# A written order for TensorE: wq's first rows by ScalarE's queue, q first, 19 exponential buffers and another list

## The chip, the cores and the metric

One core of one Trainium2 chip. Its engines are TensorE (PE in the profile, its weight loads PEld), VectorE (DVE), ScalarE (ACT), GpSimd (POOL) and SyncE (SP), which issues most transfers. The metric is the device time of one execution in microseconds, the median of several runs.

## The reference

```python
a = einsum("bsd,ed->bse", x, dft_hid_re);  b = einsum("bsd,ed->bse", x, dft_hid_im)
y = einsum("ts,bse->bte", dft_seq_re, a) - einsum("ts,bse->bte", dft_seq_im, b)
q = (x @ wq) in 32 heads of 20;  k = x @ wk;  v = x @ wv          # one k and v for all heads
p = softmax(q @ k.T * 20**-0.5);  o = (p @ v) @ wo
g = sigmoid((x * gate_w).sum(-1));  out = g * y + (1 - g) * o      # x: 2048 x 640, fp32
```

A Fourier mixing of x and an attention with 32 query heads over one shared key and value, mixed by a gate per row.

## The kernel before

All products of the first stages, of y and of o split their fp32 operands in a high and a low part (`split`) and take three products for one. The stages on TensorE are these.

1. Fifteen warm-up products (`WARM`), then `x @ [wk wv gate_w]` (tile `kv`, from `kvg`) and `x @ wq` (tile `q`), in four blocks of 512 rows of x. The first block goes chunk by chunk of 128 input features (index c): its loads alternate x and wq on SP's queue, ScalarE makes the high parts (`xh`, `wqh`), VectorE the low ones (`xl`, `wql`).
2. The hidden DFT (tile `ab`, 64 row halves, two products side by side on the two halves of the rows), with the first part of the attention's first pass between.
3. The main stage, in the order of a string `PLAN` that is written out by hand. It has three kinds of work: y, the sequence DFT, in seven products of a Strassen scheme (letters 0 and 1: the next product on the lower or the upper half of TensorE's rows); the attention's scores (letters, see below), a lower and an upper head of a pair side by side; and `V`, a step of `av`, four products of exponentials with the values on the whole of the rows. `-` empties y's bank. A letter of `SCORES` stands for a kind (a to f: first pass on the lower half, A to F: first pass on the upper half, g to l and G to L: second pass likewise) and for one of six PSUM banks.
4. A final loop for the last y groups and the rest of the second pass, then `o @ wo` with the gate and the output.

The first pass (`a_unit`) computes scores, and VectorE takes their row maxima (`mx`). When both heads of a pair are through, `a_reduce` and `a_final` come one and two ticks later, a tick being given at every second first-pass score of the list. `a_final` turns the maxima (`mt`, VectorE), splits them (`ms`, GpSimd), writes them to DRAM (`m_d`) and reads them back by four transfers into two extra rows per head of `qs`, the lower head's two first. The second pass (`b_unit`) multiplies with these rows, so its scores come with the maximum taken off; ScalarE makes the exponentials into one of 16 buffers (`pt`), which `pick` chooses while the program is built, and a step of `av` frees four of them.

SP's order is found by a scheduler; TensorE, ScalarE, VectorE and GpSimd follow the program's order. GpSimd (late in the kernel VectorE) sums and splits the DFT matrix (`split_c`).

For the last stage `load_o(n)` loads a block of 256 rows of `oT_d` and of the reciprocals `rx_d`, `mult_o` multiplies them on GpSimd, `split_o` splits them, and `o_group` takes the products.

Of the kernel before, what the change touches and what calls it, by code (L numbers as in the profile page):

```python
# [8 lines left out]
F32 = mybir.dt.float32  # L9
# [8 lines left out]
P = 128  # L18
# [12 lines left out]
WARM = 15  # L31
# [3 lines left out]
def kernel(  # L35
# [60 lines left out]

    nc.scalar.activation(gate, ident[:, :NT], AF.Exp)
# [64 lines left out]
    with ExitStack() as c1:  # L162
# [4 lines left out]
        nc.gpsimd.dma_start(kvg, wkvg.rearrange("(c p) n -> p c n", p=P))  # L167
# [590 lines left out]
    ptfree = [(-1, k) for k in range(16)]  # L758
# [82 lines left out]
    def finish_last(ts, sm):  # L841
# [20 lines left out]
        "B0A00K00F00CBjVV1e1g11d11l1c11h1e11a1j111f1h111c1-kJVHa1l1e11c1d11h11a1l11k1VHcDlAeVVCh1d1l11g1e11h1"
        "1c1l11d11gVHe0I0F00G0D00B0VIeGfDhVVhE0I0A00F00J000H0E00I00A0J000F0H00K00C0A00J0B00L00E0I000D0A000L0B"
        "iVVElj11c1g11b1l11e11d11i11g11h1l1e11c1-VdEaHcLVVDh1e1l11g1c11h111d1l11k1a111c1h11d111l1k1a1Hc1VLdKh"
        "AcVVfH0D0K00G0I00B00F0K00D0VVkAH00C00L0J00E0G00B00C00L00E0J000B00G0F00I00J00E00A0B0I00lDVVKc1a1l11h1"
        "1d1k11c1f11a111h11d1k11i1-VVBfKaIjVBk1i1f11j1a11k11h11c11l11d11a11k11h1c1f11d11KgVHkCfGdVVB00K00G0C0"
        "0L00D0B0K00G00I0F0D000E00B0A00LiVVDlI00E00H00A0L0J000C00E0H00A0L000C0D00BkVVFgIk1d111b1g11f11c1j111k"
        "1h111a1f11j1V-CaKbJlVk11c1j11a11l1h11e11c1d1GlV1e1h11c1g11d1l11e11b1iGVD0fIeB0A0VVJc0L0E000H0G00D00I"
        "00F0K00B0DgVVF00I00B0K00G0D00F00I00H0E00G00J00C0F00B0E000G0iJV1l1a11h1c11j11e11f1g11b1iDVVeGiFhJVe11"
        "fAi1b11j1-VIej11l11a111b1i1e111j1a1l11h11c1j11k11l1a11b1VcJaKlBVVdL0I0E00A0H00L00D0I00K0VViB0K0A0F00"  # L870
        "J00I00H00E0A000J0F0I00K00H00D00A000I0F00E0D00B0gCVV1f1g11e1j11b1i111l1a11k11d11i1h11f-AVVdKfIaHVdK1f"
        "1i11h11a11k1d1i11l111b1g11e1d11i11f1h111aKViDfBkAVViD00K0F00H0G00C0D00K0F000B0IaVViEJ00F0H00G00C0E00"
        "J0F00H000I00A000J0E00H0F00I00A0D00kHVVFh1c1g11e1j11b111l1a11i1j111e1l11h1VaE-cJfHVVaJ1e1h11i1l11d1g1"
        "11b11k1c1d111l1b11a111i11e1LjVIlBaDeVVlC0B0G00J0E0F00C00G0H00D0VVkA00L0B00I00D0Eg0L000B00I0D00G00K0F"
        "00C0H00G000J0K00F00B0CaVVj11f11k1b11i11a11j11lk111i11b1d11-GfVVKbIgDlVbKi11d11a11l1k11b11i1j111f1a11"
        "1k11b1i11d11l1eGVbDcFaKVVhED00I00L00A0H00E000I0J00L00B0A000I0E000J0H00F0aIVVjEF00H0A00I000J0E00H0F00"
# [24 lines left out]
        "E0G00C000F00J0E00H00I00A0J0L00B00E0C000gJVVJb1f1k11a1i111j1h111e1f11c111a1j11kHVFcJeGbVV-Fj1c11g1e1h"
        "111j1f11g1i11b1k111d11f111a1i11h1kDVfAiBkDVViFA00K0H00J00C0F00E0G00B000I0D00FaVVE00I00B0J00F00G0K00C"
        "0B00J00G00L0E00C0D000H00A0kFVVc11h1e11j1a11l11i11b1e11d1f11gi11h1-VeGdIhLVVaIh11e1l111d11i111a1h11e1"
        "1l1d11i1a11b1f111k1IjVVJaK00B00I0F00J00G0E00H00I00FdVEgFhDiVVGeF00H0D0i0G000E0H00F0I00D00G000H0E00I0"
        "0LA000J00HE00C0AfVV1e1j11c11h1a11l1k11d11i1h111a11f1kDVIhKa-LdVVi11gBdKf1VIb1g1d11k11f1c11h11g111j1e"
# [185 lines left out]
```

## Time and profile before

| | |
|---|---|
| time, median of 3 runs | 1775.57 us (1775.42 to 1776.12) |
| the profiled execution | 1775.38 us, its span 1773.6 us |
| busy: PE, PEld | 1766.9 us, 1263.0 us |
| busy: DVE, ACT, POOL | 1422.8 us, 1186.8 us, 820.1 us |
| mean granted clock of TensorE | 1.00 |

Times in the profile run from the span's start. Matmuls overlap, their ends are modelled, and the two halves of TensorE's rows work side by side, so two starts on the same half say more than a duration. A row "x4" merges several instructions. "<-" behind an idle time names what ended it.

### The profile page before, as it was taken

To read this page: it belongs to the slowest core of one execution; us is meant where nothing else is said; L and a number is where in the kernel's file an instruction comes from. 1 tells how busy PE (TensorE), PEld (TensorE's weight loads), DVE (VectorE), ACT (ScalarE), POOL (GpSimd) and SP (SyncE) were. 2 spreads that over 40 slices of the span, in tenths; PEclk is the share of its full clock that TensorE was granted. 3 is DMA by queue.
4 is the path that set the end of the run, shared out by engine and by line. 5 is a ranking of instruction groups with operands and counts; after the bars stand their busy time and mean duration, and the time that the engine had idled before them with its cause. 6 is when DMAs were issued, how large, how long until landed. Compare 5 with 4: busy or idle time off the path is not lost.

```text
span 1773.6 us, 40756 instructions
## 1 busy us (share of the span) xinstructions
PE 1766.9 (100%) x16354; PEld 1263.0 (71%) x16354; DVE 1422.8 (80%) x2335; ACT 1186.8 (67%) x2327; POOL 820.1 (46%) x560
## 2 busy tenths in 40 slices
PE   9999999999999999999999999999999999999999
PEld 7799986666666666666666666666666666667789
DVE  4469999888888898888888888888888898854344
ACT  4422247777777777777777777777777777777731
POOL 1001227454455465655766565565654454442242
PEclk9999999999999999999999999999999999999999
DMA  8762324333334442524544444353443242325666
GB/s 269 234 196 93 118 98 133 108 130 100 114 111 152 115 134 93 173 92 146 171 136 131 156 130 133 100 151 106 141 140 113 86 121 85 105 69 188 196 223 208
DMA packets 130393, 243.87 MB, mean 137 GB/s; under 512 B 25716, under 2 KB 76916, under 8 KB 127684
## 3 DMA queue, kind: packets, MB, share of 16 engines
q1 hardware_dynamic: 129356, 237.89, 42.7%
q0 software_dynamic: 848, 3.38, 0.6%
q8 instruction: 128, 2.10, 0.5%
q14 instruction: 61, 0.50, 0.1%
HBM read 194.62 MB, written 50.86 MB: 138 GB/s over the span
## 4 chain that ended last, share of the span: by engine, by line
PE 98%; DMA 1%; DVE 0%; ACT 0%; SPq 0%; issue 0%; POOL 0%; POOLq 0%; DVEq 0%; ACTq 0%
PE av L798 27%; PE y L655 21%; PE b L784 17%; PE a L329 17%; PE ab L122 7%; PE o L111 1%; PE o L112 1%; PE o L113 1%; PE q L111 1%; PE q L113 1%; PE q L112 1%; DMA x_d<-both 0%; DMA ql_d<-ql 0%; DMA kvg<-in_wkvg_dram 0%; PE kv L210 0%; PE kv L211 0%
## 5 line engine op out<-in xcount | busy, mean ns | idle before, releaser
L336 DVE TENSOR_REDUCE mx<-a 128x1 f32<-128x512 f32 x2048 | 1265.0, 683 | 171.0 <-PE a L329 111.7
L794 ACT ACTIVATE pt<-b 128x512 f32<-128x512 f32 x2048 | 1052.1, 618 | 327.1 <-PE b L784 194.8
L655 PE MATMUL y<-x,ch 64*128 64x320 f32 x3584 | 757.8, 309 | 0.0
L329 PE MATMUL a<-ks,qs 60*128 60x512 f32 x2048 | 736.2, 422 | 0.2 <-DVE mx L336 0.2
L784 PE MATMUL b<-qs,ks 62*128 62x512 f32 x2048 | 706.0, 421 | 0.5 <-ACT pt L794 0.3
L655 PEld LDWEIGHTS y<-x,ch 64*128 64x128 f32 x3584 | 559.3, 185 | 22.1 <-issue 9.4
L655 PE MATMUL y<-x,cl 64*128 64x320 f32 x1792 | 514.3, 308 | 0.0
L798 PE MATMUL av<-pt,vsb 128*32 128x512 f32 x4096 | 502.9, 600 | 0.0
L329 PEld LDWEIGHTS a<-ks,qs 60*128 60x128 f32 x2048 | 350.0, 184 | 128.0 <-DVE mx L336 98.3
L784 PEld LDWEIGHTS b<-qs,ks 62*128 62x128 f32 x2048 | 340.1, 184 | 130.3 <-ACT pt L794 70.8
L458 POOL TENSOR_TENSOR craw<-craw 128x1024 f32<-128x1024 f32 x80 | 191.2, 2390 | 269.3 <-DMA craw<-in_cre_dram 113.6
L655 PEld LDWEIGHTS y<-x,cl 64*128 64x128 f32 x1792 | 307.9, 184 | 3.8 <-issue 2.5
L798 PEld LDWEIGHTS av<-pt,vsb 128*32 128x32 f32 x4096 | 106.6, 108 | 201.1 <-issue 179.4
L463 POOL TENSOR_TENSOR cl<-craw,ch 128x1024 fp32r<-128x1024 f32 x98 | 234.6, 2394 | 7.9
L462 POOL CAST ch<-craw 128x1024 fp32r<-128x1024 f32 x98 | 101.7, 1038 | 143.4 <-PE y L655 120.2
L122 PE MATMUL ab<-wh,xh 64*128 64x320 f32 x640 | 137.0, 307 | 0.2 <-DVE both L533 0.2
L122 PE MATMUL ab<-wl,xh 64*128 64x320 f32 x640 | 136.7, 306 | 0.0
L122 PE MATMUL ab<-wh,xl 64*128 64x320 f32 x640 | 136.4, 305 | 0.0
L532 ACT ACTIVATE half<-ab 128x320 f32<-128x320 f32 x64 | 28.1, 439 | 115.4 <-PE ab L122 111.4
L711 POOL TENSOR_TENSOR ya<-yt,ya 128x320 f32<-128x320 f32 x64 | 57.4, 912 | 97.5 <-ACT yt L684 96.8
L122 PEld LDWEIGHTS ab<-wh,xl 64*128 64x128 f32 x640 | 99.7, 184 | 0.0
L122 PEld LDWEIGHTS ab<-wl,xh 64*128 64x128 f32 x640 | 99.5, 185 | 0.0
(89 smaller groups left out, 1077.2 us busy)
## 6 DMA issues: line engine op xcount, KB each, us to landing
craw<-in_cre_dram SPq DMA_DIRECT2D x96, 512.0 KB
craw<-in_cim_dram SPq DMA_DIRECT2D x96, 512.0 KB
xr<-x_d SPq DMA_DIRECT2D x88, 320.0 KB
qs<-qh_d SPq DMA_DIRECT2D x64, 160.0 KB
x_d<-both SPq DMA_DIRECT2D x64, 160.0 KB
ya<-y_d SPq DMA_DIRECT2D x64, 160.0 KB
y_d<-ya SPq DMA_DIRECT2D x64, 160.0 KB
xr<-in_xT_dram SPq DMA_DIRECT2D x20, 256.0 KB
```

The source lines that it names most:

```text
L111: nc.tensor.matmul(ps, wh, xh, start=(i == 0), stop=False)
L122: nc.tensor.matmul(ps, w[r], x[r], start=(i == 0 and k == 0), stop=(i == n - 1 and k == 2))
L329: nc.tensor.matmul(ps, qs[p][b : b + 60, qb * P : (qb + 1) * P], ks[b : b + 60, c * ROW : (c + 1) * ROW], start=True, stop=True,)
L336: return nc.vector.tensor_reduce(mx[p][:, hh, qb, c : c + 1], ps, axis=AX.X, op=ALU.max)
L458: eng.tensor_tensor(raw, raw, raws[1], op=PRODUCTS[n][0][1])
L462: eng.tensor_copy(h, raw)
L463: eng.tensor_tensor(l, raw, h.bitcast(F32), op=ALU.subtract)
L655: mm = nc.tensor.matmul(ps[g % len(ps)], w, x, start=start, stop=stop)
L711: nc.gpsimd.tensor_tensor(ya, yt, ya, op=how)
L784: nc.tensor.matmul(ps, ks[b : b + 62, kc * P : (kc + 1) * P], qs[p][b : b + 62, qc * ROW : (qc + 1) * ROW], start=True, stop=True,)
L794: halves.scored(nc.scalar.activation(t, ps, AF.Exp, scale=SCALE), n)
L798: nc.tensor.matmul(ps[32 * g : 32 * g + 32, :], vsb[:, kc, :], t, start=first, stop=last)
```

## The change

In the first stage, wq's first chunk is loaded by ScalarE's queue, ahead of the early Exp; kvg is loaded by SP's queue behind x's first chunk, in place of GpSimd's. wqh and wql are made ahead of kvg's halves, and q's products stand ahead of kv's. Twelve warm-up products instead of fifteen. There are 19 buffers of exponentials instead of 16, and `PLAN` is another string of the same length, with the same number of letters of each kind. The reciprocals of odd blocks no longer have a tile of their own: those of block 1 go in two halves into `xr0` and `xr1`, with two multiplications, those of blocks 3, 5 and 7 into `ab71`.

```diff
--- before.py
+++ after.py
@@ -28,7 +28,7 @@
 SJ = NT // 2
 SCALE = float(DH) ** -0.5
 ROW = 512
-WARM = 15
+WARM = 12
 @with_exitstack
@@ -94,8 +94,6 @@
     gate = const.tile([P, NT], F32, name="gate")
     omg = const.tile([P, NT], F32, name="omg")
-    nc.scalar.activation(gate, ident[:, :NT], AF.Exp)
-
     def words(ap):
         return ap.bitcast(F32) if ap.dtype == F32R else ap
@@ -164,7 +162,6 @@
         x1 = c1.enter_context(tc.tile_pool(name="x1", bufs=2, side="right"))
         rot = Rot(["B", "V", "F", "B", "F", "A", "A", "A"])
         kvg = w1.tile([P, KC, 41], F32, name="kvg")
-        nc.gpsimd.dma_start(kvg, wkvg.rearrange("(c p) n -> p c n", p=P))
         kvgs = w1.tile([P, KC, P], F32R, name="kvgs")
@@ -246,21 +243,24 @@
         wqraw = w2.tile([P, KC, D], F32, tag="wl1", name="wqraw")
+        move(wqraw[:, 0], wq_v[:, 0], nc.scalar)
+        nc.scalar.activation(gate, ident[:, :NT], AF.Exp)
         load_x1(0, 0)
+        move(kvg, wkvg.rearrange("(c p) n -> p c n", p=P))
         pkv = rot("kv_0")
         pq = [rot(f"q_0_{m}") for m in range(KC)]
         for c in range(KC):
             if c:
                 load_x1(0, c)
-            move(wqraw[:, c], wq_v[:, c])
+                move(wqraw[:, c], wq_v[:, c])
         for c in range(KC):
             split_x1(0, c)
+            split(wqraw[:, c], wqh[:, c], wql[:, c])
             if c == 0:
                 split(kvg, kvgs[:, :, :41], kvgs[:, :, 64:105])
-            split(wqraw[:, c], wqh[:, c], wql[:, c])
-            kv_mm(pkv, 0, c)
             for m in range(KC):
                 q_mm(pq[m], 0, m, c)
+            kv_mm(pkv, 0, c)
         for c in range(KC):
             load_x1(1, c)
         for c in range(KC):
@@ -576,17 +576,26 @@
         if n < NO:
             oraw[n] = []
             for k, v in enumerate((oT_v, rx_v)):
-                if (n % 2, k) == (1, 1):
-                    t = op.tile([P, KC, TW], F32, name="oraw", bufs=1)
+                ts = slice(n * TW, (n + 1) * TW)
+                if (n, k) == (1, 1):
+                    t = [xp.tile([P, KC, P], F32, tag=f"xr{q}", name="oraw") for q in range(2)]
+                    for q in range(2):
+                        move(t[q], v[:, :, ts][:, :, q * P : (q + 1) * P])
                 else:
-                    t = abp.tile([P, KC, TW], F32, tag=f"ab{5 + 2 * (n % 2) + k}0", name="oraw")
-                move(t, v[:, :, n * TW : (n + 1) * TW])
+                    tag = f"ab{5 + 2 * (n % 2) + k}0" if (n % 2, k) != (1, 1) else "ab71"
+                    t = abp.tile([P, KC, TW], F32, tag=tag, name="oraw")
+                    move(t, v[:, :, ts])
                 oraw[n].append(t)
     def mult_o(n):
         if n < NO:
             o, r = oraw[n]
-            nc.gpsimd.tensor_tensor(o, o, r, op=ALU.mult)
+            if n == 1:
+                for q in range(2):
+                    ts = slice(q * P, (q + 1) * P)
+                    nc.gpsimd.tensor_tensor(o[:, :, ts], o[:, :, ts], r[q], op=ALU.mult)
+            else:
+                nc.gpsimd.tensor_tensor(o, o, r, op=ALU.mult)
     def split_o(n):
         if n < NO:
@@ -755,7 +764,7 @@
-    ptfree = [(-1, k) for k in range(16)]
+    ptfree = [(-1, k) for k in range(19)]
     known = {"PE": -1, "ACT": -1, "y": -1}
     last = {}
@@ -854,96 +863,96 @@
     SCORES = "abcdefABCDEFghijklGHIJKL"
     PLAN = (
-        "1aH1Id1k11f1a11h1111id1El11h1111i1g1Df1hKVDiG0B0F000KC00J00G0B00K0000F00J0C00gE0H00dFVVg11cHeD1lVgC0"
-        "0H00E0F00J0G000C0H00E0J000L0G00C00H0eDVVcLe111g1h11d11l1i11a11e1h11d111f1a1i11bK-VViKj11lAb1Vi11a11k"
...
-        "i1d11g11k11l1c11h1g11j11eV0C00L0E00B0G000C0J00L00E0G00B0D000IlVVV0L0K000G0H0000000L0K00I000G0H0000L0"
-        "0JkVVi11g11h1k11lJi1VVVj11i11g11111J11I11-"
+        "g1Hc11d1k11l11a11c1h1Je11Fg11b11i1j111KaVfI0D0K00H00G00C0L00E00J0B000I000A0E00LjB0ViAlEjBVa11lCe1JbV"
+        "0G0F00I0D00K00B0G00L0C00D00K00A0H00L00CVVd1k11a11h1l11c1d11k1g11h11f11c1k1d11a1-VVhFc1Kd1g1VHf1k11c1"
...
+        "111c11j11g1h11l1e11i11dVE00G00D00H0F00I0K00A00D0H00I0F00K00A000B0J00I0L00K0VV0J00I00L0000K0J00G0I000"
+        "LVVK1h1j111g11i1k11l11h1VV1k1l11j1h11g1VV-"
     )
     STEPS = [(p, qh, kc) for p in range(NPAIR) for qh in range(2) for kc in range(NT)]
```

## Rows read from the trace of the kernel before

**Rows 1.** The page's part 4, the chain that ended last, shares by engine

```profile
PE 98%; DMA 1%; DVE 0%; ACT 0%; SPq 0%; issue 0%; POOL 0%; POOLq 0%; DVEq 0%; ACTq 0%
```

**Rows 2.** Groups by line: busy us, mean ns, idle before and its releasers

```profile
L794 ACT ACTIVATE pt<-b 128x512 f32<-128x512 f32 x2048 | 1052.1, 618 | 327.1 <-PE b L784 194.8 <-PE a L329 119.8 <-PE y L655 5.6
```

**Rows 3.** Timeline of the first 9 us: start, duration, instruction, idle before it

```profile
1.36 5.20 PE L244 MATMUL warm<-ident 128*128 128x128 f32 x30 [1.36 <-POOL ident masks.py:199]
...
4.62 0.63 ACT L106 ACTIVATE xh<-xr 128x512 fp32r<-128x512 f32 x1 [2.38 <-DMA xr<-in_xT_dram]
...
6.79 0.38 ACT L106 ACTIVATE kvgs<-kvg 128x205 fp32r<-128x205 f32 x1 [1.54 <-DMA kvg<-in_wkvg_dram]
...
7.08 0.72 ACT L106 ACTIVATE wqh<-wqraw 128x640 fp32r<-128x640 f32 x1
...
7.83 0.82 DVE L107 TENSOR_TENSOR wql<-wqraw,wqh 128x640 fp32r<-128x640 f32 x1 [0.25 <-ACT wqh L106]
...
8.71 0.50 PE L113 MATMUL q<-xh,wql 128*128 128x512 f32 x1
```

**Rows 4.** Stretches at the start: busy time by engine, granted clock, DMA share, GB/s

```profile
2.00:3.00 1.00, 1.00 (x6) 1.00 (x6) 0.00 (x0) 0.23 (x2) 1.00 (x2) 1.00 0.77 151
...
3.00:4.00 1.00, 1.00 (x7) 1.00 (x6) 0.00 (x0) 0.00 (x0) 1.00 (x2) 1.00 0.71 208
...
4.00:5.00 1.00, 1.00 (x8) 1.00 (x7) 0.00 (x0) 0.38 (x1) 1.00 (x2) 1.00 1.07 368
```

**Rows 5.** Timeline 15 to 24 us: the last wql, and the last rows' first product

```profile
15.58 0.83 DVE L107 TENSOR_TENSOR wql<-wqraw,wqh 128x640 fp32r<-128x640 f32 x1 [0.25 <-ACT wqh L106]
...
23.75 0.40 PE L210 MATMUL kv<-xh,kvgs 128*128 128x512 f32 x1
```

**Rows 6.** Timeline of TensorE, 803 to 811 us, in the written list

```profile
803.23 1.92 PE L798 MATMUL av<-pt,vsb 128*32 128x512 f32 x16
...
806.36 0.39 PE L784 MATMUL b<-qs,ks 62*128 62x512 f32 x1
...
806.51 0.31 PE L655 MATMUL y<-x,ch 64*128 64x320 f32 x1
...
806.59 0.39 PE L329 MATMUL a<-ks,qs 60*128 60x512 f32 x1
...
806.65 0.31 PE L655 MATMUL y<-x,ch 64*128 64x320 f32 x1
...
808.59 1.06 PE L798 MATMUL av<-pt,vsb 128*32 128x512 f32 x8
...
809.58 0.50 PE L329 MATMUL a<-ks,qs 60*128 60x512 f32 x2
```

**Rows 7.** Timeline of TensorE where the written list ends

```profile
1594.38 0.71 PE L784 MATMUL b<-qs,ks 62*128 62x512 f32 x2
...
1595.58 0.50 PE L784 MATMUL b<-qs,ks 62*128 62x512 f32 x2 [0.28 <-ACT pt L794]
```

**Rows 8.** Timeline 1042 to 1055 us: the chain of pair 9's row maxima

```profile
1042.70 0.50 PE L329 MATMUL a<-ks,qs 60*128 60x512 f32 x1
...
1045.85 0.20 DVE L350 STREAM_TRANSPOSE mt<-mxr 128x32 f32<-128x32 f32 x1
...
1046.69 0.32 SPq L103 DMA_DIRECT2D m_d<-ms  x1
...
1049.45 2.49 SPq L103 DMA_DIRECT2D qs<-m_d  x4
...
1054.46 0.39 PE L784 MATMUL b<-qs,ks 62*128 62x512 f32 x1
```

**Rows 9.** Timeline of SP's queue, 1494 to 1503 us: pair 14's maxima

```profile
1496.48 0.32 SPq L103 DMA_DIRECT2D m_d<-ms  x1
...
1497.94 2.51 SPq L103 DMA_DIRECT2D qs<-m_d  x4
```

**Rows 10.** Page part 5: GpSimd's sum of two blocks of the DFT matrix

```profile
L458 POOL TENSOR_TENSOR craw<-craw 128x1024 f32<-128x1024 f32 x80 | 191.2, 2390 | 269.3 <-DMA craw<-in_cre_dram 113.6
```

More of the change, by code (lines that the diff above doesn't have):

```diff
@@ L862 @@
[L862 to L876, printed above, removed]
@@ L902 @@
[L902 to L905, printed above, removed]
-        "111f1h11c1a11jEVVH00F00J0C00G00E0H0L00D00I0A00bEVVlD0I00A0H00E000L0D00I0G00B0E00L00J0I00A00H0F00E00J"
@@ new lines @@
+        "1g1c11e1LhVgLD00H00C0K00A0VdLhCkAVVdH0K0F00I00A0B00J0E00L00I000A00J000L0B000I0E00J0A00L0B00C00E00J0F"
+        "gVVHd1c11g1e11l1b11j11a11c11l1k11d11h1Vl-KaHcDVVAl1c1k1h11d111f1g11k11c11h1d11a1l111k1i11b11fJVVaBkI"
+        "fJVkA0B0I000J00F0E00G00CbD0VVgF0K0C00H0D00A00L0K000C0H00D0L000A00K0B00I00L00D00E0G0C00hFVVJa1b1k11i1"
+        "1f1j11a1e11h111c11l1j11a1V-VBlJeIaVBl1e11j11i1a11l11b1j11e1i1111a1l11b1j111e1c1LgVbJlEaCVVD00L0H00E0"
+        "0G0C0000L0D00H00E0G00I0F0D00H0kAVVFiH000D0K0A000I0F00H0J00E0A00C00F000B0jKVVaKd11i1111lB1k11ai11j11f"
@@ new lines @@
+        "1b11e11a11i1dLV-VIb1k1f11a11j1i11b11k1l111d11g11c1b111e1fJVVcGjBeLVg11c1BjFkVgC0B0J00K0fG00C00D0H00K"
+        "000L0A00ChVV0D0K000A0L00H00C0K00D0A00L0B00I00K00J0L00A00I00BeVAj1l1i11b11k1j11a11f1b11i1VkAfJiBVa11f"
+        "1e11j1B-cVVJaf11k1h11c1j11g11k1f111h1c11j11a11l11e1i11b1VjLgEiBVeJ0L0B00A0I00J00E0L00B0VVVIaJ00E00L0"
+        "B00I0G00D0E00L000B00I0D00G00L000E00I0B00G0D00F0kCVVAh1d1k11l11c11h1a11e11j11f1c11h11g1Vj-HeGfCVVe1Hd"
+        "111g1l11c11h1e11a1j11f1i11h1k111d11a1c11HlVKhDaFiVVHe0I00D0G000F0H0K00C00D0A00F0H00iEVVhDI00A00F0K00"
@@ new lines @@
+        "H0D00I000G0K00F0H000D00C00G0L00E00dBVVC1g1e11l1d11h11i1a11k1l11b11d1i11a1VbK-lDcGVVbK1l1d11g11c1k111"
+        "b1l11d1g11c1k111b111l1a11dKi1VlKbAcDVVlB0K0G00C00J0F000B0E00C00A0LjVVB00J00E0L00I0A00B00J00K0L00C0A0"
+        "0J0B00E00I000F0GjVI00G0bJeLV1b1i11e1a11j1f11h11i1e11d111a1b11l-CVVl11e11j1a11h11i1f11k1d1GhV1iFk1d11"
+        "g11h1i11f11e11dGVHiFeDgVVIg0B00L0E00D0I00H00A000E0L00I0J00B000A0F00E0I00hJVViAH00F00J00E0I0A00H0F00D"
+        "000K00I0AbVVfKd11i11g11bk11f1i111d11g11h1e11l11cV-GhDeLiVVd1Gh1e11f11i1j11a111h11e1i1l11d111a1h11e1i"
@@ new lines @@
+        "11fJVaHeCjFVVA00H0E00J00C00L00A0B0E00D0LiVVLaB00I00K00J00F0A000I0B00K0F00J000I0A0K00B00J00L0C00AeVVB"
+        "jLia1111k1d11b1l111g11c1d11k11h11f1G-cVdFeHgCVVd11h11f1g11k11c1d11h1f11g11e1i111hj11g1f11c1VhEfDcGVV"
+        "bK0G0F0J000C00K0H00A0L0J00I0VVhE00L0A00J0I00B0E000L00A0J00B0I00F0K00D00G0C0000B0E0lAVV1d11l1c11h11e1"
+        "g11d1l111h1c11e1g11l-DVVHcEgDfVVIb1g1k11d1f11i11b11g11j11e1l111c1a11h1j11k11fVHcJ00A0K00F00H00C0J000"
+        "A0K0lB0VjKcAlBVVJc0K0A00B0L00J00C00K0G000F0B00J000K00I0A00F0D000B0K0GiVKgFdBcVVKf1a11j11b1i11k11f1d1"
@@ new lines @@
+        "1a11i1h11e11f1VV-cHj11a1e11l11h1i11d1g111f11e1h11j11i111a1f1Bk1VaFdIkBVVA00K00I0F00J0B00A0E00I00L0J0"
+        "0B0ViAlEjBVA00I00E0L00J0B000I0A00K0F00J00B00I0A00K00F0J00bCVV1a1k11j1f11b11i1a11k1d11f11c1h11e1-VVAh"
+        "d11l11i1e111b1g11l1d111c11k1g11b1f1111d1k1gIVKbGfJiVVjE0B0I00G0F00J00K0C0B00G0VjKfCgBVVJf0kC0G00B00J"
+        "0L000E00I0A00B00J0E00L00C0G00J0B00L000E00A0iJVVJf1b11i11e1g11d11l11c1b11a11k1l11j1VKl-CbDaVVcKl11b1j"
+        "11a11k1c11l11h1d11g111e1c11l11h11j1a1EVCaLhDkVVhC0K00F00G0D00H00C00E0F00GdH0VVHc0G0E00L00D0H0I00A00K"
@@ new lines @@
+        "0F00D00H000A0I00K00F00H0D000C0gEVV1fHd1g11i111e11h1f11g11j1i11k1b11f1VbGjCfKVV-bGc111j1e11l111g1b11j"
+        "1i11f111g1e11b11j1i11f1GeVVbJiFgEVJbI00F00E0G00J0H000C00F0G00E0J000I00B0G00F0D00E0VViBG000F0J00E00I0"
+        "0H0A00F0D0K000C0AhVVFk1j1b11c1g111l1e111d1h111a11c11f1kHVV-dKhAcLVk11d11h1a11l1c11k11j1h1a11l111e1i1"
+        "1d11g11b1kFVIdBaKfVVId0K0B00G0L00C00J0E00B0A0000I0F0kJVViBA00K00J00F0I00H00E0A000J00F0I00K0B00D00A00"
+        "0I0FkVVBi1j11e1a11l11c1h1j111k1f1g1h11c11d1VfKg-CdHVVfKc11h1g11d11e11l1b11i11g1j111f1k1111c1a11b1dLV"
```

122 lines of the change are left out of this document (56 added, 66 removed).

## The prediction

> **What bounds the kernel now.** I read the chain that ended last first. The reader is to see that TensorE holds 98% of it, while ScalarE and VectorE stand at 0%: the kernel ends when TensorE has streamed its list [rows 1]. So an edit is worth only what it takes from or adds to TensorE's own time: its late start, its order, or a wait put into it. Next I read who ended ScalarE's idle time before the exponentials. It is the scores themselves (194.8 us), the first pass (119.8) and y (5.6), which is 320.2 of 327.1 us; av, whose end frees a buffer, is not among them [rows 2]. So a lack of buffers can have held ScalarE for 6.9 us at most, in its own slack. Then I read the first nine microseconds as a timeline, the spacing of TensorE's work in the middle, the point where the written list ends, and the chain of the row maxima.
>
> **The start.** TensorE's real work waits for kvg: ScalarE converts it at 6.79 after 1.54 us of idling for its transfer, wqh follows at 7.08, wql at 7.83, and the first product with wql starts at 8.71, with kv's two and q's first two ahead of it [rows 3]. After the change wq's first rows come by ScalarE's queue, are converted right behind x's, and q goes first. x's conversion starts at 4.62. Then 0.63 + 0.72 (wqh) + 0.82 (wql) + 0.06 (end of wql to its product, 8.65 to 8.71) puts that product at 6.85 [rows 3]. It then has two products fewer ahead of it, at 0.23 each (the 512 columns of a score take as long [rows 6]), so the list as a whole moves up by 8.71 - 6.85 - 0.46 = 1.40 us. That is the upper end: x's first rows must not land later although wq's now travel beside them.
>
> The lower end: x's and wq's first rows are 262 and 328 KB. By the bytes moved, 151 KB up to 3.0, 208 more up to 4.0 and then 368 in a microsecond, x's alone are through at 3.53 and both at 4.63 [rows 4]. x's conversion began 1.09 after 3.53. If both land together, it begins at 5.72 and 0.30 us is left. I take 1.1, nearer the upper end, because wq's rows may come 0.63 us behind x's at no cost. The Trainium skill (DMA: Bandwidth & Descriptors, section "Issuing engines are not separate DMA queues") says that transfers started by different engines share the same 16 DMA engines and interleave, so a second queue saves only the time of issuing. It speaks for the lower end: by it the gain of the start would be 0.3, and by the rows of x's landing alone 1.4.
>
> What hides the rest: ScalarE's issue and the early Exp stand before 4.62, where ScalarE idles. kvg now rides second in SP's queue, where wq's first rows were; nobody needs its halves before fifteen q products from about 6.4 are through, at 9.8, against 6.79 when it came now, so 3 us of cover; beyond that it costs one to one, since ScalarE converts it ahead of all later x and wq. SP issues as many transfers as before, and GpSimd is free of one. The last rows' wql is ready at 16.41 and used from 23.75 [rows 5], so an earlier TensorE does not run into it. Twelve warm-ups instead of fifteen: thirty records in 5.20 us [rows 3], 24 of them end about 1.0 earlier, some 5.5. A gap of about 0.9 us to the first product stays, shorter than today's (6.56 to four products ahead of 8.71, 7.8), and the granted clock reads 1.00 in all these stretches [rows 4]; I cost it at nothing. If the clock fell, some 15 products would take twice 0.23, 3.5 us. Behind the start TensorE has no gap to swallow the gain: it stays.
>
> **The list.** Both lists hold the same letters by kind (1,888 first-pass scores, 1,920 second-pass, 4,608 y, 478 steps of av), so only the order counts. I walk down each: a y occupies its half of the rows for 0.147 us (0.14 by two starts, 0.147 over longer runs), a score for 0.235, the halves run side by side, and none starts before its predecessor [rows 6]. Between the av blocks the old list needs 821.9 us and the new one 820.8: -1.1. A step of av costs 0.86 (1.92 for two steps against 1.06 for one), and a block 0.99 from its start to the next score [rows 6], so at least 0.13 on top of the step, and some 0.2 more to drain the scores ahead of it: 0.34 a block. The new list has 298 blocks against 296: +0.7. Sum -0.4; with the durations taken a few per cent longer or shorter it stays within -0.2 to -0.8. The Trainium skill (TensorEngine Tiling (Array Packing), "Key Properties") says that a change of tiling mode drains the engine; the trace agrees with 0.99 for a block whose step costs 0.86, and it is what speaks against the two added blocks.
>
> 19 buffers in place of 16: by [rows 2] nothing by themselves. They let the list hold up to 19 exponentials open (16 before), which is how it may be ordered otherwise.
>
> **The end of the list.** Behind the old list's last av block come scores on banks whose exponentials aren't through: of the final loop's first four scores the first starts at about 1594.60 (the second of two that span 0.71, one taking 0.49) and the last two at 1595.58, released by ScalarE [rows 7]. Two pairs side by side would start their second pair 0.24 behind the first, so 0.7 is lost. The new list ends on an av block, behind which ScalarE has caught up. I take -0.7; bounds 0 and -1.0.
>
> **The chain of the maxima, the cost that I see in the new list.** A pair's second pass may begin only when its row maxima have gone DVE, GpSimd, DRAM, and back into qs; the last link is issued by a tick, which the list gives at every second first-pass score, so two ticks behind the last one. For pair 9 of the old list: last first-pass score at 1042.70, second tick 1.5 later by the walk (1044.2), mt 1045.85, m_d issued 1046.69, four qs issues from 1049.45 to 1051.94, and the first score that needs the last of them at 1054.46, unhindered [rows 8]. From tick to last issue 7.8 us; over eleven pairs 6.3 to 7.9, median 7.5 (this pair is at the long end; the pair of [rows 9] needs 7.0). The landing takes 1.1 to 2.4 more, by how long m_d's takes before SP goes on [rows 8, 9], and 2.5 at most, as pair 9 didn't wait.
>
> Walking both lists from that tick to the first score needing it: the old one never leaves less than 10.0 us (pair 9), then 10.3 and 10.5. The new one leaves 7.1 for pair 9 and 6.9 for pair 10, and in both it is the second head, whose rows are issued last. The walk runs up to 0.3 short. So 7.4 and 7.2 stand against 7.5 + 1.1 to 2.4: TensorE waits 1.2 to 2.5 and 1.4 to 2.7 us, and everything behind is queued in order, so it is paid in full. With the shortest link chain (6.3 + 1.1) it is 0.2 in all, with the longest 5.9. I take 1.6 + 1.8 = +3.4.
>
> **The last stage.** Block 1's multiplication by the reciprocals goes from one operation 1,280 columns wide to two of 640 on GpSimd (1,024 columns take 2.39 us [rows 10], so about 3.0 in sum either way), and its loads from two to three. Its product is wanted only behind four output groups of fifteen products each, 8.8 us at y's 0.147 (both are 320 columns); that covers it, so I cost it at nothing. Without the cover it would be the 3.0 us of the multiplication, at most.
>
> **Sum** against the profiled execution's own 1775.38 (span 1773.6; 0.2 below the median 1775.57): -1.1 - 0.4 - 0.7 + 3.4 = +1.2, 1776.6.
>
> **Rivals.** (a) The maxima arrive in time: SP goes on behind m_d's issue as soon as in [rows 9], 1.3 us earlier than for pair 9, with a short queue on VectorE. Then the waits are gone: -2.2, 1773.2. For it: the old pair 9 was met without a wait. Against: two pairs, both 3 us tighter than any before. (b) Faster: (a), with each of the other three terms at its favourable end (-1.4, -0.8, -1.0), and the new order also sparing delays of some tenths that the walk doesn't see: 1772.2 and below, to 1770. For it: the start alone can give 1.4. Against: it needs all of them. (c) Slower: GpSimd is in the middle of its own work when the maxima reach it. One of its operations takes 2.39 us [rows 10], so one ahead of the cast in each of the two pairs adds 4.8: 1781.4. It decides if GpSimd's order has a split of the DFT matrix just ahead of the cast; the list puts the last ones 6.6 and 12.5 us before the tick, which speaks against it. (d) wq's first rows, travelling beside x's, hold these back to the full 1.09 us: start -0.3 in place of -1.1, 1777.4. This is the sharing of engines that the Trainium skill states in the section named above.
>
> **How the numbers follow.** Forecast 0.42, (d) 0.10, (a) 0.25, (b) 0.13, (c) 0.10. A measurement here tells about 0.2%, 3.55 us, from no change: the forecast, (a) and (d) lie within, (b) mostly below, (c) above, and a little of (a) falls to (b)'s side. So faster 0.16, same 0.73, slower 0.11. The range leaves out (b)'s far part and (c): 1772.0 to 1779.5, the upper end being the long end of the waits (+5.9 in place of +3.4).
>
> **What the profile would show.** Start: first q at about 6.3 instead of behind kv, TensorE gapless behind it. List: scores of pairs 9 and 10 near 1050 and 1140 held with qs's transfer as releaser, 1 to 3 us each; without them I am wrong by the +3.4. The final loop's first scores without ScalarE's wait. The forecast also fails if the first products run at half clock, or kvg lands behind 9.8.

## The result, and the profile after

The changed kernel takes 1778.08 us (median of 19 runs, 1776.90 to 1780.33), the kernel before beside it 1775.78 (19 runs, 1775.27 to 1777.75): a ratio of 1.0013, 95% interval 1.0007 to 1.0019. That is within the 0.2% that the prediction named as no change, and 1.5 above the forecast of 1776.6 (+2.3 against the kernel before beside it, where +1.2 was forecast). The profiled executions are 1777.61 after (span 1775.8) and 1775.38 before. Of the terms behind that sum one has the wrong sign and is 2.4 us off, and others came out lower than forecast (waits and list, by 0.8 and 0.5); the experiments are about these. The times after also scatter more (3.4 us from lowest to highest, 2.5 before).

The page after, as before, has TensorE as the end of nearly everything, and ScalarE still waits for scores, y and the first pass, not for buffers (its row in the view by line answers to [rows 2]: 326.1 of 331.7 us). New is the wait in the last row: b's scores held by the transfer of the row maxima.

```profile
PE 97%; DMA 1%; DVE 1%; SPq 0%; POOL 0%; issue 0%; ACT 0%; DVEq 0%; POOLq 0%; ACTq 0%
...
L803 ACT ACTIVATE pt<-b 128x512 f32<-128x512 f32 x2048 | 1052.2, 619 | 331.7 <-PE b L793 184.7 <-PE a L329 133.6 <-PE y L664 7.8
...
L793 PE MATMUL b<-qs,ks 62*128 62x512 f32 x2048 | 702.0, 422 | 2.6 <-DMA qs<-m_d 2.4
```

The start, which answers to [rows 3]: x's conversion is held from 4.62 to 5.11 by wq's rows beside it, and the first product with wql starts at 7.29 in place of 8.71. With two products of 0.23 fewer ahead of it, the list moves up by 8.71 - 7.29 - 0.47 = 0.95 (forecast 1.1). This differs by some tenths from trace to trace: the first product with wql starts at 8.71 to 9.16 in the six traces with the old start and at 7.24 to 7.92 in the eight with the new one. The warm-ups end at 6.42, not at the forecast 5.5: their 24 records take 5.06 us where thirty took 5.20 before, at a granted clock of 1.00 in both. So they end 0.15 ahead of the first product, and there is no gap of 0.9.

```profile
5.11 0.63 ACT L104 ACTIVATE xh<-xr 128x512 fp32r<-128x512 f32 x1 [2.42 <-DMA xr<-in_xT_dram]
5.65 0.72 ACT L104 ACTIVATE wqh<-wqraw 128x640 fp32r<-128x640 f32 x1
...
6.40 0.83 DVE L105 TENSOR_TENSOR wql<-wqraw,wqh 128x640 fp32r<-128x640 f32 x1
...
7.29 0.50 PE L111 MATMUL q<-xh,wql 128*128 128x512 f32 x1
```

Forty microseconds later it is gone. In the same view of TensorE, block 2's kv products, which ran at one every 0.233 from 48.10 to 50.20 before, stop twice: from 48.77 to 50.38 and from there to 51.33, where 0.23 each would do: 2.1 us are lost, and 0.1 more at the transpose behind.

```profile
48.54 0.40 PE L207 MATMUL kv<-xh,kvgs 128*128 128x512 f32 x1
48.77 0.40 PE L208 MATMUL kv<-xl,kvgs 128*128 128x512 f32 x1
50.38 0.49 PE L207 MATMUL kv<-xh,kvgs 128*128 128x512 f32 x1 [1.21 <-ACT xh L104]
51.33 0.50 PE L208 MATMUL kv<-xl,kvgs 128*128 128x512 f32 x1 [0.45 <-DVE xl L105]
51.76 0.44 PE L228 MATMUL kvt<-ident,kvT 41*128 41x41 f32 x4
```

ScalarE and SP, 26 to 50 us, tell why. Block 0's kv ends behind q's last product now; its eviction starts at 26.95 (24.41 before), and everything that follows in order is 2.5 to 3 us later than before: SP's six small copies into ks, then the stores of q, whose landing frees q's buffers (the wait of 5.38, which the kernel before has too, with 5.42: it is not longer now, only later), then the conversions, w's rows, and at 49.72 the last of block 2's x (46.76 before). TensorE itself comes to that point at about 49.0.

```profile
26.95 0.59 ACT L215 ACTIVATE kvT<-kv 41x512 f32<-41x512 f32 x1 [8.87 <-PE kv L208]
...
28.99 0.91 SPq L101 DMA_DIRECT2D ks<-kh  x1
...
33.87 0.42 SPq L101 DMA_DIRECT2D qh_d<-qh  x1
...
36.40 0.60 ACT L200 ACTIVATE qh<-q 128x512 fp32r<-128x512 f32 x1 [5.38 <-DMA qh_d<-qh]
...
49.08 0.74 ACT L104 ACTIVATE wh<-wraw 128x640 fp32r<-128x640 f32 x1 [1.00 <-DMA wraw<-in_wrT_dram]
49.72 0.61 ACT L104 ACTIVATE xh<-xr 128x512 fp32r<-128x512 f32 x1
```

The rows of the kernel before that these answer to:

```profile
24.41 0.60 ACT L218 ACTIVATE kvT<-kv 41x512 f32<-41x512 f32 x1 [5.57 <-PE kv L211]
...
46.76 0.62 ACT L106 ACTIVATE xh<-xr 128x512 fp32r<-128x512 f32 x1
...
49.97 0.39 PE L210 MATMUL kv<-xh,kvgs 128*128 128x512 f32 x1
50.20 0.40 PE L211 MATMUL kv<-xl,kvgs 128*128 128x512 f32 x1
```

So the hidden DFT starts at 90.31 (89.06 before): the start cost +1.25 where -1.1 was forecast.

The chain of pair 9's maxima, 1044 to 1057 us, answers to [rows 8]: from the last first-pass score to mt 3.8 us, to m_d's issue 0.8, to the first qs issue 2.8, four issues 2.5, and 1.6 behind the end of the last one the first score of head 1, which has stood 1.12. Pair 10's stands 1.25 (the last row). Against a walk of the letters, as in the prediction, these two stretches are 1.35 and 1.28 too long, an estimate: +2.6 for a forecast of +3.4.

```profile
1044.48 0.50 PE L329 MATMUL a<-ks,qs 60*128 60x512 f32 x1
...
1048.32 0.20 DVE L350 STREAM_TRANSPOSE mt<-mxr 128x32 f32<-128x32 f32 x1
...
1049.15 0.32 SPq L101 DMA_DIRECT2D m_d<-ms  x1
...
1051.91 2.50 SPq L101 DMA_DIRECT2D qs<-m_d  x4
...
1056.01 0.47 PE L793 MATMUL b<-qs,ks 62*128 62x512 f32 x1 [1.12 <-DMA qs<-m_d]
...
1146.41 0.47 PE L793 MATMUL b<-qs,ks 62*128 62x512 f32 x1 [1.25 <-DMA qs<-m_d]
```

The end of the list, which answers to [rows 7]: av's last block ends the list at 1597.8, and the final loop's first four scores follow without a wait for ScalarE, as forecast.

```profile
1596.01 1.92 PE L807 MATMUL av<-pt,vsb 128*32 128x512 f32 x16
1597.86 0.74 PE L793 MATMUL b<-qs,ks 62*128 62x512 f32 x4
```

From the end of the hidden DFT to the last stage it is 1448.1 before (249.39 to 1697.49) and 1449.1 after (250.73 to 1699.84): +1.0. With +2.6 for the waits, -1.6 is left for list and end together (forecast -1.1). The last stage takes 72.4 in both, from its first product to its last.

### The profile page after: what moved, and what is told of

It reads as the page before. It is cut to its first block, busy times and chain, and to the rows that moved or that the text cites. A ratio compares the mean times of both kernels' runs of the same rounds, so it can differ in the third digit from the quotient of the medians.

```text
span 1775.8 us, 40733 instructions
## 1 busy us (share of the span) xinstructions
PE 1766.4 (99%) x16348; PEld 1259.9 (71%) x16348; DVE 1427.8 (80%) x2335; ACT 1186.8 (67%) x2327; POOL 823.0 (46%) x560
## 4 chain that ended last, share of the span: by engine, by line
PE 97%; DMA 1%; DVE 1%; SPq 0%; POOL 0%; issue 0%; ACT 0%; DVEq 0%; POOLq 0%; ACTq 0%
PE av L807 27%; PE y L664 21%; PE b L793 17%; PE a L329 16%; PE ab L120 7%; PE o L109 1%; PE o L110 1%; PE o L111 1%; PE q L109 1%; PE q L111 1%; PE q L110 1%; DMA ql_d<-ql 0%; SPq L101 0%; DMA x_d<-both 0%; PE warm L241 0%; POOL craw L458 0%
## 5 line engine op out<-in xcount | busy, mean ns | idle before, releaser
L803 ACT ACTIVATE pt<-b 128x512 f32<-128x512 f32 x2048 | 1052.2, 619 | 331.7 <-PE b L793 184.7
```

The lines of the kernel that those rows point to most:

```text
L803: halves.scored(nc.scalar.activation(t, ps, AF.Exp, scale=SCALE), n)
```

## The experiments

The change has two halves that touch nothing of each other, so each was taken alone first, and then each suspected cost was taken out or made larger. All times are medians; the kernel before ran beside each group, at 1775.18, 1775.25 and 1775.18.

**The start alone** (the old list, 16 buffers and the old last stage; the change's edits of the first stage).

```
-WARM = 15
+WARM = 12
...
+        move(wqraw[:, 0], wq_v[:, 0], nc.scalar)
...
-            kv_mm(pkv, 0, c)
             for m in range(KC):
                 q_mm(pq[m], 0, m, c)
+            kv_mm(pkv, 0, c)
```

> The start's edits alone (wq's first rows by ScalarE's queue, q's products ahead of kv's, twelve warm-ups), with the old list and 16 buffers. Theory, from the two traces: with kv's products last, block 0's kv ends 2.5 us later, and so does everything that ScalarE and SP do behind it; TensorE then loses 2.2 us in block 2 at kv's products, whose x splits are late, and the start as a whole costs +1.3 (about 1777.1 against 1775.8 of the kernel before). Rival, the step of the prediction: TensorE has no gap behind the start to swallow the gain, so it is -1.0 (1774.8), and what is lost in block 2 comes from something else.

Measured: 1777.34 (11 runs, 1775.93 to 1778.49), ratio 1.0010 (1.0002 to 1.0019), +2.2. The trace has the same two waits in block 2 (1.13 and 0.45). The rival, that the gain stays, falls. The runs stand in two groups, five at 1775.93 to 1776.28 with a mean clock of 1.000 and six at 1777.34 to 1778.49 with 0.999, about 1.6 apart, which the expectation didn't foresee. The profiled execution is of the first group.

**The list alone** (the old start; 19 buffers, the last stage's loads, the new list).

```
-    ptfree = [(-1, k) for k in range(16)]
+    ptfree = [(-1, k) for k in range(19)]
...
     PLAN = (
...
```

> The new list, the 19 buffers and the last stage's loads alone, with the old start. Theory: the waits of pairs 9 and 10 for the maxima (2.6 us together) less what the list and its end give (1.6): +1.0, about 1776.8, with the two waits in the profile at the first score of head 1 or thereabouts. Rival: the waits have to do with the later start, and the list alone gives -1.6.

Measured: 1775.78 (1775.46 to 1776.46), ratio 1.0004 (0.9995 to 1.0013), +0.6. The interval holds 1, so the size is rough; the waits are read from the trace. They are there without the new start, 1.15 and 0.92 of standing at the first scores; the rival falls. All its runs have a clock of 1.000.

```profile
1055.02 0.47 PE L793 MATMUL b<-qs,ks 62*128 62x512 f32 x1 [1.15 <-DMA qs<-m_d]
...
1145.13 0.47 PE L793 MATMUL b<-qs,ks 62*128 62x512 f32 x1 [0.92 <-DMA qs<-m_d]
```

**The start with kv early.**

```
             split(wqraw[:, c], wqh[:, c], wql[:, c])
...
+            if c == KC - 1:
+                kv_mm(pkv, 0, c)
             for m in range(KC):
                 q_mm(pq[m], 0, m, c)
-            kv_mm(pkv, 0, c)
+            if c < KC - 1:
+                kv_mm(pkv, 0, c)
```

> The start's edits alone, but in the last chunk of block 0 kv's two products stand ahead of q's fifteen triples, so that kv ends as early as in the kernel before. Theory (late kv): the stall in block 2 goes away and the 0.95 us by which TensorE starts earlier stays: -1.0, about 1774.8; first-pass scores and ab start 1.0 earlier than in the kernel before. Rival (the stall comes from ScalarE's queue or from TensorE being early, not from kv): block 2's stall of some 2 us stays, +1.3.

Measured: 1774.09 (1773.59 to 1774.60), ratio 0.9993 (0.9984 to 1.0002), -1.1; the interval just holds 1, but all eleven runs lie below the lowest of the kernel before (1774.82). Two products moved by 3.5 us are worth 2.0 us against the shorter runs of the start alone (1776.06), 3.3 against its median. In its trace kv of block 2 runs through and the last x is converted 3.8 earlier than in the changed kernel:

```profile
45.89 0.61 ACT L104 ACTIVATE xh<-xr 128x512 fp32r<-128x512 f32 x1
...
48.97 0.40 PE L207 MATMUL kv<-xh,kvgs 128*128 128x512 f32 x1
49.20 0.39 PE L208 MATMUL kv<-xl,kvgs 128*128 128x512 f32 x1
```

**The buffers alone** (old list, 19 buffers, the last stage's loads).

> The old list with 19 buffers of exponentials and the last stage's changed loads, nothing else. Theory: nothing waits for a buffer in the old list, so 0.0 (within 0.3). Rival: a buffer's release holds ScalarE, and through it the banks of the scores: up to -2, seen as fewer waits of scores for ScalarE.

Measured: 1775.39 (1774.98 to 1776.16), ratio 1.0001 (0.9993 to 1.0010). Nothing, as [rows 2] said.

**The list alone, with the maxima's chain issued at once for pairs 9 and 10.**

```
         if u % 64 == 63:
-            later(1, a_reduce, u // 64)
-            later(2, a_final, u // 64)
+            if u // 64 in (9, 10):
+                a_reduce(u // 64)
+                a_final(u // 64)
+            else:
+                later(1, a_reduce, u // 64)
+                later(2, a_final, u // 64)
```

> The new list alone (as in the second experiment), but for pairs 9 and 10 the reduction, the transpose and the rest of the chain of the maxima are issued directly behind the last first-pass score, not one and two ticks later. mt then starts some 2 us earlier, and the last rows land before the first score that needs them. Theory: the two waits, 1.4 and 1.0 us in the second experiment's trace, go away: about 2.3 less than that experiment, 1773.4. Rival (the waits only show another bound, ScalarE's exponentials or the banks behind them): the wait changes its releaser, and the time stays within 0.5 of the second experiment's 1775.8.

Measured: 1774.04 (1773.47 to 1774.73), ratio 0.9990 (0.9981 to 0.9999), 1.7 below the list alone. Pair 9's wait is gone; pair 10's is 0.20, its first score again 1.6 behind the end of the last issue. What is left of the new list is -1.2 against the kernel before.

**The list alone, with that chain two ticks later.**

```
+            n = 2 if u // 64 in (9, 10) else 0
-            later(1, a_reduce, u // 64)
-            later(2, a_final, u // 64)
+            later(1 + n, a_reduce, u // 64)
+            later(2 + n, a_final, u // 64)
```

> The new list alone, with the chain of the maxima of pairs 9 and 10 issued two ticks later than in the changed kernel. Theory: a chain that is already late passes any further delay on in full. VectorE alone would start mt some 2.7 us later (four reductions of 0.6 to 0.7): +5.4 over the second experiment, 1781; and if the cast then falls behind GpSimd's three operations of a split of the DFT matrix (2.4 us for the first, at 1048.07 in the second experiment's trace), up to 7 a pair, +14. Rival (there is slack in the chain, or the score waits for something else as well): clearly less than 2 a pair.

Measured: 1784.80 (5 runs, 1783.92 to 1786.62), ratio 1.0050 (1.0036 to 1.0063), 9.0 above the list alone. The waits themselves grew as VectorE's delay alone had it, from 1.15 and 0.92 to 3.56 and 3.71, +5.2 in all; GpSimd was not in the way (its cast at 1049.93, the split of the DFT matrix behind it at 1050.43). The other part is TensorE's clock. The profiled execution, the longest of the five (1786.62), shows it. Columns of these stretches: busy time of PE, PEld, DVE, ACT and POOL, granted clock, DMA share, GB/s.

```profile
1054.00:1055.00 1.00, 0.00 (x0) 0.00 (x0) 0.33 (x1) 0.36 (x1) 0.92 (x2) 1.00 0.85 311
1055.00:1056.00 1.00, 0.00 (x0) 0.00 (x0) 0.00 (x0) 0.00 (x0) 1.00 (x1) 1.00 0.60 204
1056.00:1057.00 1.00, 0.00 (x0) 0.00 (x0) 0.00 (x0) 0.00 (x0) 1.00 (x2) 0.76 0.27 54
1057.00:1058.00 1.00, 0.65 (x4) 0.68 (x6) 0.00 (x0) 0.00 (x0) 1.00 (x1) 0.50 0.51 180
...
1062.00:1063.00 1.00, 1.00 (x6) 0.65 (x4) 1.00 (x3) 0.00 (x0) 0.00 (x0) 0.50 0.97 360
1063.00:1064.00 1.00, 1.00 (x9) 0.41 (x12) 1.00 (x3) 0.60 (x1) 0.00 (x0) 0.82 0.85 330
1064.00:1065.00 1.00, 1.00 (x12) 0.14 (x7) 0.39 (x1) 0.00 (x0) 0.00 (x0) 1.00 0.06 26
```

TensorE stands from 1053.8 to 1057.35; its clock falls from 1.00 to 0.50 while it stands and comes back only at about 1063.2, six microseconds after the work did. The stretch of pair 9 is 6.3 us too long by the walk, of which 3.56 are the wait itself; pair 10's is 6.2, of which 3.71.

```profile
1057.35 0.76 PE L794 MATMUL b<-qs,ks 62*128 62x512 f32 x1 [3.56 <-DMA qs<-m_d]
...
1153.02 0.76 PE L794 MATMUL b<-qs,ks 62*128 62x512 f32 x1 [3.71 <-DMA qs<-m_d]
```

**The changed kernel with kv early, and with both edits.**

> The changed kernel with one edit: in the last chunk of block 0, kv's two products stand ahead of q's. Theory, from the first and third experiments: block 2's stall goes and the start's gain comes out, so -1.1 from the start and +0.6 from the list on the 1775.2 of the kernel before: 1774.7; and the scatter of the changed kernel's times (3.4 us between its runs, with a mean clock of 0.999 in the longer ones) goes with the stall. Rival: the new list's own waits grow when it starts earlier, and the scatter belongs to the list: 1776 or more, still scattered.

Measured: 1775.07 (1774.49 to 1775.79), ratio 0.9998 (0.9989 to 1.0006). That is nearer to the theory (1774.7) than to the rival (1776 or more). Its runs, all with a clock of 1.000, spread over 1.3 us; those of the kernel before at that clock, beside it, over 1.6.

> The changed kernel with both edits: kv ahead of q in the last chunk, and the chain of pairs 9 and 10 issued directly. Theory: the terms add, -1.1 (start), -1.7 (list without its waits): 1772.4 against 1775.2, the fastest of all, without scatter. Rival: a later stage swallows a part (the last tick's DMAs, ScalarE), and it is no better than the better of the two edits, about 1773.5.

Measured: 1773.04 (1772.37 to 1774.54), ratio 0.9986 (0.9977 to 0.9995), -2.2: better than both kernels and than either edit alone. It is less than expected, but what the terms measured singly add up to (-1.1 for the start with kv early, -1.2 for the list with its waits mended), so nothing is swallowed later.

**kv last, alone**, in the kernel before (only the order of the last chunk's products).

```
-            kv_mm(pkv, 0, c)
+            if c < KC - 1:
+                kv_mm(pkv, 0, c)
             for m in range(KC):
                 q_mm(pq[m], 0, m, c)
+            if c == KC - 1:
+                kv_mm(pkv, 0, c)
```

> The kernel before with one edit: in the last chunk of block 0, kv's two products stand behind q's fifteen; everything else of the start is as it was. Theory: kv ends 15 products of 0.233 later, 3.5 us; block 2's last x split, ready 1.9 before it is needed in the kernel before, comes 1.6 late, so TensorE loses 1.6 to 1.9 us in block 2 and the time is 1776.9 against 1775.2. Rival: the stall of the start's edits needs the earlier TensorE or the changed queues as well, and this edit alone is 0.

Measured: 1778.55 (1777.01 to 1779.52), ratio 1.0017 (1.0008 to 1.0026), +3.4, more than expected. Four runs with a clock of 1.000 at 1777.0 to 1777.6 are near the expected stall (+1.8 to +2.4 for 1.6 to 1.9); seven with 0.999 lie 1.6 higher. The profiled execution is one of these, and shows where. TensorE in block 2:

```profile
49.79 0.40 PE L211 MATMUL kv<-xl,kvgs 128*128 128x512 f32 x1
51.57 0.50 PE L210 MATMUL kv<-xh,kvgs 128*128 128x512 f32 x1 [1.38 <-ACT xh L106]
52.51 0.49 PE L211 MATMUL kv<-xl,kvgs 128*128 128x512 f32 x1 [0.44 <-DVE xl L107]
...
54.45 0.63 PE L112 MATMUL q<-xl,wqh 128*128 128x512 f32 x1
...
57.75 0.39 PE L111 MATMUL q<-xh,wqh 128*128 128x512 f32 x1
```

Stretches of the same trace (busy time of PE, PEld, DVE, ACT and POOL, granted clock, DMA share, GB/s):

```profile
52.00:54.00 2.00, 1.56 (x9) 1.11 (x9) 1.06 (x2) 0.00 (x1) 0.54 (x1) 1.00 0.96 333
54.00:56.00 2.00, 2.00 (x7) 1.57 (x6) 0.00 (x0) 0.24 (x1) 0.00 (x0) 0.55 1.07 269
56.00:58.00 2.00, 2.00 (x7) 1.53 (x7) 1.47 (x3) 1.21 (x3) 0.36 (x1) 0.60 0.94 352
58.00:60.00 2.00, 2.00 (x10) 1.64 (x9) 1.30 (x4) 1.93 (x4) 0.18 (x1) 1.00 0.68 200
```

After the stall, q's products follow each other by 0.43 instead of 0.233, seven full spacings and one in part at either end, from 54.1 to 57.75: 7 x 0.194 + 0.11 + 0.08 = 1.55 us longer in sum, about what the two groups of runs are apart. The granted clock of 54 to 56 us is 0.55 there, of 56 to 58 0.60, and 1.00 around them.

**ks by GpSimd's queue**, in the start alone, block 0's six copies only.

```
+                queue = nc.gpsimd if n == 0 else nc.sync
-                move(ks[r0 : r0 + 20, ts], kh)
+                move(ks[r0 : r0 + 20, ts], kh, queue)
...
```

> The start's edits with kv late as in the change, but block 0's six small copies into ks are issued by GpSimd's queue and not by SP's, so that SP goes on to q's stores at once. Theory of the link (a late kv acts through SP: its six issues, 4 to 5 us in all, stand ahead of the stores that free q's four buffers, whose next use holds ScalarE and VectorE): block 2's stall goes though kv ends as late as before, -1.0, 1774.2. Rival link (ScalarE's own wait for kv's end, ahead of all of q's evictions): the stall stays near 2 us, +0.7 and more, 1776 to 1778.

Measured: 1775.66 (1774.59 to 1776.84), ratio 1.0002 (0.9993 to 1.0011): between the two. The first link is shown: SP goes on to q's stores at 30.22 (34.05 in the start alone), and the wait ahead of q's fifth eviction, 5.40 on ScalarE and 5.53 on VectorE there, is down to 1.06 and 2.29. But block 2's stall is still 1.9 us in the trace, because w's first rows now stand behind the copies in GpSimd's queue (issued at 33.40, at 4.04 in the start alone), and ScalarE waits for them instead. This execution is the longest of the eleven (1776.84): x's conversion starts only at 5.75 in it and the first product with wql at 7.92, so it gained 0.3 at the start; no trace of a shorter one is kept. ScalarE and GpSimd:

```profile
32.73 0.60 ACT L200 ACTIVATE qh<-q 128x512 fp32r<-128x512 f32 x1 [1.06 <-DVE ql L201]
...
33.40 1.10 POOL L101 DMA_DIRECT2D wraw<-in_wrT_dram  x2
...
40.80 0.74 ACT L104 ACTIVATE wh<-wraw 128x640 fp32r<-128x640 f32 x1 [2.63 <-DMA wraw<-in_wrT_dram]
```

So the edit put a new wait in the place of the one that it took away, and how much of the stall SP's copies alone account for stays open.

**kv later still**, in the start alone: the last two of block 0's kv products behind block 1's ten.

```
...
+            if c < KC - 1:
+                kv_mm(pkv, 0, c)
...
+        pkv1 = rot("kv_1")
+        for c in range(KC):
+            kv_mm(pkv1, 1, c)
+        kv_mm(pkv, 0, KC - 1)
         kvT = kv_out(pkv, 0)
...
```

> The start's edits with kv of block 0 later still: its last two products stand behind the ten of block 1's kv, 2.3 us further back. Theory: the chain is already late, so the whole 2.3 shows in block 2, a stall of 4.5 in place of 2.2, and 1775.9 + 2.3 = 1778.2 at full clock; and if the mean clock of 0.999 in the longer runs of the first experiment comes from that stall, the granted clock of TensorE in the trace falls from 1.00 to 0.50 behind it, in more or all runs, for some us more (1779 to 1782). Rival: the stall has another bound (the loads of the next weights), and it stays near 2 us with the clock at 1.00.

Measured: 1778.73 (9 runs, 1778.38 to 1780.87), ratio 1.0023 (1.0013 to 1.0033). Five runs at a clock of 1.000 have 1778.38 to 1778.73, 2.4 above those of the start alone: the size is right, the place only in part. The profiled execution pays it in two places, 1.40 at block 1's transpose, which needs kv's eviction, and 1.81 in block 2 (1.58 in the start alone). Four runs have 0.999 and lie 1.9 higher; that is not more of them than in the start alone (six of eleven), though more or all were expected, and since the trace is of a run with 1.000 it can't show where they lose it.

**wq's first rows by SP's queue**, behind x's, in the start with kv early.

```
-        move(wqraw[:, 0], wq_v[:, 0], nc.scalar)
         nc.scalar.activation(gate, ident[:, :NT], AF.Exp)
         load_x1(0, 0)
+        move(wqraw[:, 0], wq_v[:, 0])
```

> The start's edits with kv early (the third experiment), but wq's first rows issued by SP's queue right behind x's first rows, in place of ScalarE's. Theory, by the traces: beside wq's rows x's conversion began 0.49 later (5.11 against 4.62); behind them it begins at 4.62 again, and wq's rows, through at about the same time, are converted at 5.7 to 5.9 as before: within 0.3 of the third experiment, 1774.1. Rival: a second queue saves its whole issue time, and without it the first products start 0.6 to 0.7 later, 1774.8.

Measured: 1773.92 (1773.75 to 1774.31), ratio 0.9993 (0.9984 to 1.0002), -1.3 against the kernel before, where ScalarE's queue gave -1.1. x's conversion starts at 4.63 again, wq's at 5.53, and the first product with wql at 7.32, against 7.24 with ScalarE's queue. In this trace it no longer waits for wql, which is ready at 7.12: the warm-ups end only at 6.64 and put q's first product at 6.79.

```profile
4.63 0.63 ACT L104 ACTIVATE xh<-xr 128x512 fp32r<-128x512 f32 x1 [2.38 <-DMA xr<-in_xT_dram]
5.53 0.74 ACT L104 ACTIVATE wqh<-wqraw 128x640 fp32r<-128x640 f32 x1 [0.27 <-DMA wqraw<-in_wq_dram]
...
7.32 0.39 PE L111 MATMUL q<-xh,wql 128*128 128x512 f32 x1
```

The gain of the start thus comes from q's going ahead of kv and kvg, with three warm-ups fewer (these two were not taken apart); the second queue adds nothing that shows. What it does to x is seen in every trace: x's conversion starts at 5.07 to 5.75 in the seven traces with wq's first rows on ScalarE's queue, and at 4.54 to 4.75 in the seven without. The Trainium skill (DMA: Bandwidth & Descriptors, "Issuing engines are not separate DMA queues") says that transfers started by several engines interleave on the same 16 DMA engines, and that a second queue saves only the time of issuing. The traces agree: x was held back by 0.49 us in the changed kernel.

## Why the prediction was right, and where it was not

**The total** came out within its range, but partly by luck: the start was forecast 2.4 too low, and waits and list together 1.3 too high. Forecast: -1.1 (start), -0.4 and -0.7 (list and its end), +3.4 (waits), +1.2 in all. Measured by trace: +1.3, -1.6, +2.6, some +2.3 in all. By runs: start +2.2 as a median (+0.9 at a mean clock of 1.000), list +0.6.

**The start, the step that failed**, is the sentence "Behind the start TensorE has no gap to swallow the gain: it stays." So the step took a TensorE that doesn't wait now for one that can't be made to wait. The gain as such was sized rightly: 0.95 by the trace, 1.1 by the runs with kv early. What was missed is that the same edit moves kv's last products from the head of the last chunk to its end, and with them everything that ScalarE and SP do behind kv. What the runs show in its place is a stall of 2.1 us in block 2, 2.2 with the transpose: the start cost +1.25 in the trace. I checked that TensorE doesn't run into the last wql, and that kvg isn't needed before 9.8; I did not follow kv's result downstream. By [rows 5] kv's first product of the last chunk stood at 23.75, q's fifteen behind it: 3.5 us, a number that the prediction could have had. That kv's lateness is the cause is shown from both sides: kv early alone gives the gain back, and kv late alone, without any other edit, costs 1.8 to 2.4 plus the clock. That the lateness passes through SP's copies into q's stores is shown for the first link; the rest of the way, through w's rows to x, is read from the traces. The gap of 0.9 us ahead of the first product, with the warm-ups through at 5.5, did not come either (they ended at 6.42); it cost nothing here.

**The clock** has no term in the sum: the prediction put it at nothing for the gap at the start, where it cost nothing, and had no stall for it to follow. In 9 of the 19 runs after, the mean clock is 0.998 or 0.999, and these runs are 1.4 longer (median 1778.84 against 1777.43). In no trace of the changed kernel itself is the place of it to be seen; that it is block 2's stall is inferred from the kernel with kv last alone, where it is, from the clock of 1.000 in all 44 runs of the four kernels with kv early and in the 33 of those with the old start, except the two that delay kv or the maxima. With ks by GpSimd's queue it is 1.000 in all 11 runs too, though its trace shows 1.9 us lost in block 2, so what decides between the two times stays open. Nor is the stall needed for such a run: of the 91 runs of the kernel before that stood beside the experiments, two have 0.999, at 1778.57 and 1778.61, 3.4 above the others of their group. In the changed kernel it puts the median 0.65 above that of the runs without it.

**The waits of pairs 9 and 10** were right in place and mechanism, both of them, head 1, the releaser named, and forecast 0.8 too large: by the runs they are worth 1.7 (list alone) or 2.0 (changed kernel), by the trace 2.4 to 2.6. The landing was right: 1.5 by the prediction's own numbers (7.5 + 1.5 - 7.4 = 1.6), 1.6 to 1.7 in every trace that waits. TensorE stood 1.12 and 1.25 where 1.6 and 1.8 were forecast, 0.5 less each. The term that was sized too long is the chain from the tick to the last issue. VectorE follows the program's order, and mt stands there behind the reduction of the first-pass score of 1047.17 and ahead of that of 1047.52, so pair 9's tick is at 1047.52, and pair 10's likewise at 1138.21. From there to the end of the last issue it is 6.9 and 6.6 us, where 7.5 was taken; to the place of the score, without its standing, it is 7.4 and 7.0, where the walk gave 7.4 and 7.2.

**List and end** were forecast at -1.1; the list alone without its waits gives -1.2 by runs, with 0.2 of pair 10's wait still in it. Buffers: nothing, as forecast. Last stage: nothing, as forecast.

**The rivals.** (a) and (b) needed the maxima in time; they weren't. (c), GpSimd in its own work, did not come even with the chain two ticks later. (d), x's rows held back, came by half in the changed kernel's trace, 0.49 of 1.09, and in full in one other (conversion at 5.75, with ks by GpSimd's queue). At 0.49 it lost next to nothing against wq behind x on SP's queue: there wq's rows were converted at 5.53, where they were at 5.65 after the change. The range's upper end, called the long end of the waits, is 1779.1 by the prediction's own numbers (1776.6 + 5.9 - 3.4), not 1779.5; nothing hangs on it.

## What to carry to other kernels

When an edit moves work on the engine that sets the end, follow the result of each moved instruction too, not only its operands: two products put last on TensorE delayed an eviction, six copies, eight stores and the splits of the block after next, and lost twice what the edit had gained. A chain through memory with a known length (here 6.6 to 7.8 us from its tick to the end of its last issue, and 1.6 more to the first product that needs it) is a distance that the order of work has to keep; a list ordered without it can shorten it just where it may not. And an edit that is neutral in sum may hold a gain: with the two costs taken out, the same change is 0.14% better.

## What the runs showed of the hardware

A wait of TensorE can cost more than its length, and not in every run. With waits of 3.6 to 3.7 us the granted clock fell from 1.00 to 0.50 (2.4 to 1.2 GHz) and stayed there for some six microseconds of work after it; behind waits of 1.38 and 0.44 us, with 0.5 of work between, it fell to half for 3.4 us in the execution that was profiled, and by the mean clock in 7 runs of 11. The same pair of waits in the changed kernel's trace, 1.21 and 0.45 us, left it at 1.00. Behind single waits of 0.9 to 1.25 us in the list it stayed at 1.00 in the traces of the changed kernel, of the list alone and of the changed kernel with kv early. So medians of a kernel with such a stall mix two times, here 1.6 us apart, and one profile shows only one of them.
